# Ten 256-column matmuls read in another order behind each attention product and at every second FFN step

## The chip, the cores and the metric

The kernel runs on one core of a Trainium2 chip. The metric is device time in microseconds for one execution, inputs and outputs in HBM. Times shown are medians of several executions; the profile is of one execution, whose own time stands in the table below.

## What is computed

An attention without a score matrix, then a feed-forward network. Cut to what matters:

```python
# q, k, v: (8, 8, 576, 64) float32; w_in: (512, 2048); w_out: (2048, 512)
q_s = softmax(q, axis=-1)              # over the head's 64 columns
k_s = softmax(k, axis=2)               # over the sequence
kv  = einsum('bhsd,bhse->bhde', k_s, v)
att = einsum('bhsd,bhde->bhse', q_s, kv)
x   = att.transpose(0, 2, 1, 3).reshape(4608, 512)
h   = x @ w_in
out = (h * sigmoid(1.702 * h)) @ w_out   # (4608, 512) float32
```

## The kernel before

**Tiles and blocks.** The 4,608 tokens are worked in nine blocks (t = 0 to 8) of 512. Each block goes through eight steps, and a step takes two of the 16 chunks of 128 of the FFN's inner width. The FFN's matmuls run in float32r, and each product is made of three: high x high, high x low and low x high part of the two operands.

**Two ways of multiplying.** Blocks 0 and 1 compute the first FFN product plainly, in matmuls of 512 columns (`plain1`, line 868), and blocks 0 to 2 do so for the second (`ffn2`, line 1132). From block 2 on the first product (`ffn1`, line 913), and from block 3 on the second (`ffn2s`, line 1048), are taken apart into seven smaller products in Strassen's manner; those matmuls have 256 columns. In `ffn1` the seven products of a step come in the order 1, 5, 6, 3, 7, 2, 4, and each is six matmuls: two halves of the contraction by three operand parts. In `ffn2s` each unit is also six: two row halves by three parts. So the 256-column matmuls come in groups of six on one PSUM region, with 84 matmuls to a step from block 3 on. `ffn1` has 56 steps from block 2 to block 8, which is 2,352 matmuls; `ffn2s` has 2,016.

**Attention among the FFN.** The attention of block t is computed during block t-1: `kv_pairs` multiplies k by v (line 702, matmuls of 64 or 65 columns), `q_tr` transposes q (line 757, four transposes of 128 columns), `x_pairs` applies kv to q (line 778). Where a block of 512 tokens straddles two batches of 576, `x_pairs` splits its columns in two pieces, which are laid out as four runs: a piece of 64 columns is four runs of 16, on input and output. In the plan these three kinds stand between the FFN's groups, some seven places to a block.

**The order of the work.** The order is made by a planner (`Plan`). Each piece of work is added with an engine, an assumed cost, the buffers that it reads and writes, and a rank; the planner plays this through and then emits the pieces in that order, each by calling its `run` function. TensorE is one queue, so its matmuls stand in the order in which the `run` functions were called. A matmul instruction comes with a weight load of its own (LDWEIGHTS, shown as PEld), which loads the 128 x 128 stationary operand. The moving operand is the one whose columns stream through: in `ffn1` it is a part of x, `x[:, r, c, :]`, and in `ffn2s` a part of the weights, `wx[:, r]`, both 128 x 256. The output is 256 neighbouring columns of a PSUM bank.

The other engines split operands into high and low parts (`L1030`, `L1034`), add up the products (`L936`, `L1019`, `L1076`) and apply the activation (`L942`); weights stream in by DMA issued on SyncE and GpSimd (`L411`, `L987`).

Of the kernel before, what the change touches and what calls it, by code (L numbers as in the profile page):

```python
# [136 lines left out]
def efficient_attention_then_gelu_ffn(  # L137
# [27 lines left out]
    nc = tc.nc  # L165
# [136 lines left out]
        nc.tensor.matmul(bank[Z], zeros[:, 0:P], zeros[:, 0:512], start=True, stop=True)  # L302

    plan.fill = 0.3, fill

    def R(t, step, off=0.0):
        return SLOTS * (NS * t + step) + off
# [206 lines left out]
    def parts(t):  # L514
        b, s0 = divmod(t * TB, S)
        n = min(TB, S - s0)
        got = [(b, s0, 0, n // C)]
        if n < TB:
            got.append((b + 1, 0, n // C, P))
        return got  # L520
# [160 lines left out]
    def kv_pairs(b, hps, t, rank):  # L681
        bk = next_bank(t)
        pk = bank[bk][:, : len(hps) * W].rearrange("p (m w) -> p m w", w=W)
        nr[0] += 1
        r = rs[nr[0] % 2][:, : len(hps)]
        reads = ["kl", "vl", "kl0", "vl0", "vt0"]
        for hp in hps:
            reads += [("kt", hp), ("kl", hp), *(early_tile("v", hp)[1] if b == 0 else (("vt", hp),))]

        def run():  # L690
            for m, hp in enumerate(hps):
                vx = early_tile("v", hp)[0] if b == 0 else vt[hp]
                for cols in (slice(0, D), slice(D, W)) if b == 0 else (slice(0, W),):
                    for c in range(CM + 1):
                        for a in range(2):
                            lhs = kt[hp][:, a, c, :] if c < CM else kl[:, 2 * hp + a, :]
                            if c == CM:
                                rhs = vl[:, 2 * hp + a, cols]
                            else:
                                rhs = vl[:, 0, cols] if cols.start == D else vx[:, a, c, cols]  # L700
                            r0 = (a ^ (hp % 2)) * D
                            nc.tensor.matmul(  # L702
                                pk[r0 : r0 + D, m, cols], lhs, rhs, start=c == 0, stop=c == CM, tile_position=(0, r0)
                            )

        def run_r():
            nc.vector.tensor_scalar_add(r, pk[:, :, D], 1e-9)
            nc.vector.reciprocal(r, r)

        PB, RK = ("bank", bk), ("r", nr[0] % 2)  # L710
        plan.add("PE", 0.57 * len(hps) + 0.36, reads, (PB,), rank, run)
        plan.add("DVE", 0.35, (PB,), (RK,), rank, run_r)
        for m, hp in enumerate(hps):

            def run_n(m=m, hp=hp):
                nc.scalar.mul(kvn[b % 2][:, hp, :], pk[:, m, 0:D], r[:, m : m + 1])

            plan.add("ACT", 0.35, (PB, RK), (("kvn", b % 2, hp),), rank, run_n)
# [31 lines left out]
    def q_tr(t, hp, rank):  # L750
        bk = next_bank(t)
        pq = bank[bk]
        qx, QK = q_ready(t, hp)

        def run():
            for c in range(C):
                nc.tensor.transpose(pq[:, c * P : (c + 1) * P], qx[:, c], ident)  # L757

        PB, Q = ("bank", bk), ("qT", hp % 2)
        plan.add("PE", 0.45, (QK, "ident"), (PB,), rank, run)  # L760
        plan.add("ACT", act(TB), (PB,), (Q,), rank, lambda: nc.scalar.copy(qT[hp % 2], pq))

    def x_pairs(t, half, rank):
        hps = (2 * half, 2 * half + 1)
        bks = [next_bank(t) for _ in hps]
        reads = [("qT", 0), ("qT", 1)]
        reads += [("kvn", b % 2, hp) for hp in hps for b, *_ in parts(t)]

        def run():
            for b, s0, p0, p1 in parts(t):  # L770
                for a in range(2):
                    for hp, bk in zip(hps, bks):
                        odd = hp % 2
                        ri, ro = (slice(y * D, (y + 1) * D) for y in (a ^ odd, a))
                        qx, po = (
                            y.rearrange("a (c p) -> a c p", c=C)[:, :, p0:p1] for y in (qT[odd], bank[bk])
                        )
                        nc.tensor.matmul(  # L778
                            po[ro], kvn[b % 2][ri, hp, :], qx[ri], start=True, stop=True,
                            tile_position=((a ^ odd) * D, a * D),  # L780
                        )

        PBs = [("bank", bk) for bk in bks]
        plan.add("PE", 1.2, reads, PBs, rank, run)
        for hp, bk, PB in zip(hps, bks, PBs):
            if t < 2:
                H, L = ((("place", 4 * t + hp), e) for e in "hl")

                def run_l(hp=hp, bk=bk):
                    x = xp(t, hp)  # L790
                    nc.vector.tensor_tensor(out=x[:, 1], in0=bank[bk], in1=x[:, 0].bitcast(F32), op=ALU.subtract)

                plan.add("ACT", act(TB), (PB,), (H,), rank, lambda hp=hp, bk=bk: nc.scalar.copy(xp(t, hp)[:, 0], bank[bk]))
                plan.add("DVE", dve(TB), (PB, H), (L,), rank, run_l)
                continue

            def run_c(hp=hp, bk=bk):
                nc.scalar.copy(xf(half)[:, :, hp % 2, :], bank[bk].rearrange("p (u n) -> p u n", u=2))

            plan.add("ACT", act(TB), (PB,), (("x", half, hp % 2), *taken(t, half)), rank, run_c)  # L800
# [98 lines left out]
    def ffn1(t, step):  # L899
# [4 lines left out]
        def product(n):  # L904
            bk, opens, u, at_ = PROD[n]
            K = ("wt", i, at_) if u == "T" else ("wj", i, u, at_ // 2)

            def run():
                x = xo(n)
                for c in range(2):  # L910
                    for e, (l, r) in enumerate(((0, 0), (0, 1), (1, 0))):
                        w = (wt(i)[:, at_] if u == "T" else wj[i][u][:, at_ // 2])[:, l, c * P : (c + 1) * P]
                        nc.tensor.matmul(  # L913
                            ph[bk], w, x[:, r, c, :],
                            start=opens and c == 0 and e == 0, stop=c == 1 and e == 2, skip_group_check=True,
                        )

            reads = [K, ("xs", n, "h"), ("xs", n, "l")]
            PB = ("bank", bk)
            plan.add("PE", 0.71, reads if opens else [*reads, PB], (PB,), R(t, step, OPS[n][2]), run)  # L920
# [78 lines left out]
    def ffn2s(t, G, rank):  # L999
# [23 lines left out]
        def product(n, src, b, opens):  # L1023
            s = nl[0] % 4
            old = [("gs", s // 2, s % 2, u, jj) for u in range(2) for jj in range(2)] if nl[0] < 4 else []
            nl[0] += 1
            HK, LK = ("L", s, "h"), ("L", s, "l")

            def run_l():
                nc.vector.tensor_tensor(  # L1030
                    out=L[s][:, 1], in0=x[:, :, src], in1=L[s][:, 0].bitcast(F32), op=ALU.subtract
                )

            plan.add("ACT", act(2 * HT), XK(src), (HK, *old), 0, lambda: nc.scalar.copy(L[s][:, 0], x[:, :, src]))  # L1034
            plan.add("DVE", dve(2 * HT), (*XK(src), HK), (LK, *old), 0, run_l)
            PB = ("bank", b)
            for q, p in enumerate(ps):
                if n in CHUNK:
                    K, w = ("wb", ring(n, p)), (ring(n, p), 0, 1)
                else:  # L1040
                    jj, d = {1: (0, 0), 2: (1, 0), 3: (1, 1)}[n]
                    K, w = f"wo{p}{jj}", (p, jj, d)

                def run(q=q, w=w):
                    wx = wo[w[0], w[1]][:, w[2]]
                    for h in range(2):
                        for i, (l, r) in enumerate(((0, 0), (0, 1), (1, 0))):
                            nc.tensor.matmul(  # L1048
                                bv(b)[:, h], L[s][:, l, q, h * P : (h + 1) * P], wx[:, r],
                                start=opens and q == 0 and h == 0 and i == 0, stop=q == 1 and i == 2,  # L1050
                                skip_group_check=True,
                            )

                k, done[0] = done[0], done[0] + 1
                reads = [K, HK, LK]
                plan.add(
                    "PE", 0.71, reads if opens and q == 0 else [*reads, PB], (PB,),
                    R(t, 2 * G + 2 + k // 7, UNITS[k % 7]), run,
                )
                if n in CHUNK and not end:  # L1060
                    load_u(n, pair(t, 2 * G + 2 + q), rank)
                elif n in CHUNK and t + 1 < NB:
                    pass
# [174 lines left out]
```

## Time and profile before

| what | value |
|---|---|
| median of three timed runs | 826.66 us (826.53 to 826.96) |
| the profiled execution's own time | 824.24 us |
| its span, first to last instruction | 822.5 us |
| TensorE busy | 812.3 us, 99% |
| VectorE busy | 671.6 us, 82% |
| ScalarE busy | 587.7 us, 71% |
| matmuls of 256 columns in the FFN | 4,368 |

Reading it: a matmul counts as busy from its start to a modelled end, and neighbours overlap in the pipeline, so a busy TensorE doesn't say how fast its matmuls follow one another. The recorded length of a 256-column matmul is about 0.28 us, while the next one starts about 0.12 us after it. Block 2 begins at about 217 us of the span, and block 3 at about 308 us.

### The profile page before, as it was taken

The page shows a single profiled execution, that of the slowest core. Times are in us where ns is not written, and L with a number is a line of the kernel's source. Part 1 is how long each engine was busy: PE and PEld are TensorE (multiplying, and loading weights), DVE is VectorE, ACT ScalarE, POOL GpSimd, SP SyncE. Part 2 cuts the span into 40 slices and gives each one's busy share as a digit, 9 for nine tenths or more (in the row PEclk, how much of TensorE's full clock was granted, in tenths as well). Part 3 has the DMA queues.
Part 4 walks back from the last instruction along what each step waited for, and adds up shares of the span by engine and source line. Part 5 has one row for each costly group of instructions (what it writes and reads, how often), then busy time and mean ns, then how long its engine had stood idle before and what let it go on. Part 6 is the DMA issues. An engine that isn't in the chain of part 4 may idle for free.

```text
span 822.5 us, 17452 instructions
## 1 busy us (share of the span) xinstructions
PE 812.3 (99%) x6508; PEld 740.4 (90%) x6508; DVE 671.6 (82%) x1292; ACT 587.7 (71%) x1105; POOL 248.8 (30%) x439
## 2 busy tenths in 40 slices
PE   9999999999999999999999999999999999999997
PEld 4677788877888888999999999999999999999997
DVE  8899998799568977978779988899789885686556
ACT  5798969696747796886568895889697755565442
POOL 1120121021222332553234423443343234333430
PEclk9999999999999999999999999999999999999999
DMA  9999753778399978997699868986897589768973
GB/s 280 351 339 318 260 180 128 235 244 277 111 356 270 334 233 236 308 311 217 180 256 355 248 180 233 335 275 184 233 288 222 152 235 286 224 165 247 308 230 103
DMA packets 119061, 204.06 MB, mean 248 GB/s; under 512 B 18624, under 2 KB 63680, under 8 KB 117952
## 3 DMA queue, kind: packets, MB, share of 16 engines
q0 software_dynamic: 53856, 123.23, 52.7%
q1 hardware_dynamic: 65120, 79.71, 30.9%
q8 instruction: 52, 0.85, 0.4%
q14 instruction: 33, 0.27, 0.1%
HBM read 168.30 MB, written 34.60 MB: 247 GB/s over the span
## 4 chain that ended last, share of the span: by engine, by line
PE 92%; DMA 4%; DVE 3%; issue 0%; ACT 0%; SPq 0%; DVEq 0%; ACTq 0%
PE bank L913 33%; PE bank L1048 29%; PE bank L1132 14%; PE bank L868 9%; PE bank L702 2%; PE bank L778 2%; PE bank L757 2%; DMA vl<-in_v 1%; DMA raw<-in_moe_w_out 1%; PE bank L302 1%; DMA out<-O 1%; DMA raw<-in_moe_w_in 1%; DMA qT<-in_v 1%; PE bank L650 0%; PE bank L651 0%; DVE raw L343 0%
## 5 line engine op out<-in xcount | busy, mean ns | idle before, releaser
L913 PE MATMUL bank<-xo,wt 128*128 128x256 f32 x1344 | 193.2, 280 | 0.8 <-ACT X L932 0.8
L913 PEld LDWEIGHTS bank<-xo,wt 128*128 128x128 f32 x1344 | 173.8, 188 | 7.1 <-issue 1.8
L913 PE MATMUL bank<-xo,wj 128*128 128x256 f32 x1008 | 146.2, 281 | 0.0
L1048 PE MATMUL bank<-w,gl 128*128 128x256 f32 x1008 | 140.9, 279 | 0.9 <-DVE O L1076 0.9
L1048 PE MATMUL bank<-w,gh 128*128 128x256 f32 x1008 | 141.3, 279 | 0.2
L411 POOL DMA_DIRECT2D wj<-kept x138 | 73.2, 530 | 214.1 <-PE bank L913 141.5
L913 PEld LDWEIGHTS bank<-xo,wj 128*128 128x128 f32 x1008 | 129.0, 188 | 2.1 <-ACT gl L1034 0.8
L1048 PEld LDWEIGHTS bank<-w,gl 128*128 128x128 f32 x1008 | 127.4, 188 | 1.4 <-issue 1.1
L1048 PEld LDWEIGHTS bank<-w,gh 128*128 128x128 f32 x1008 | 127.5, 188 | 0.7 <-issue 0.3
L936 DVE TENSOR_TENSOR X<-bank,X 128x256 f32<-128x256 f32 x168 | 70.3, 421 | 64.0 <-PE bank L913 60.6
L1132 PE MATMUL bank<-w,gh 128*128 128x512 f32 x384 | 119.8, 393 | 0.8 <-DVE w L379 0.8
L987 POOL DMA_DIRECT2D w<-kept_u x152 | 80.5, 530 | 124.5 <-PE bank L1048 93.5
L932 ACT COPY X<-bank 128x256 f32<-128x256 f32 x168 | 61.6, 371 | 60.0 <-PE bank L913 58.2
L942 ACT ACTIVATE X<-X 128x256 f32<-128x256 f32 x168 | 68.5, 415 | 47.1 <-DVE X L936 46.7
L868 PE MATMUL bank<-xp,wj 128*128 128x512 f32 x384 | 101.0, 397 | 0.9 <-DVE wj L379 0.7
L868 PEld LDWEIGHTS bank<-xp,wj 128*128 128x128 f32 x384 | 71.0, 188 | 20.3 <-issue 2.6
L1076 DVE TENSOR_TENSOR O<-bank,O 128x512 f32<-128x512 f32 x102 | 70.1, 687 | 15.5 <-PE bank L1048 14.8
L1132 PEld LDWEIGHTS bank<-w,gh 128*128 128x128 f32 x384 | 69.4, 188 | 14.2 <-DVE w L379 1.4
L1132 PE MATMUL bank<-w,gl 128*128 128x512 f32 x192 | 75.5, 393 | 0.0
L411 POOL DMA_DIRECT2D wt<-kept_t x84 | 44.5, 530 | 87.3 <-PE bank L913 73.5
L1019 DVE TENSOR_TENSOR X<-X 128x512 f32<-128x512 f32 x96 | 66.2, 695 | 3.7 <-ACT X L942 2.5
L1030 DVE TENSOR_TENSOR gh<-X,gh 128x512 fp32r<-128x512 f32 x84 | 57.5, 686 | 8.1 <-ACT gh L1034 7.8
(125 smaller groups left out, 1205.4 us busy)
## 6 DMA issues: line engine op xcount, KB each, us to landing
wt<-kept_t POOLq DMA_DIRECT2D x84, 512.0 KB, 6.0
w<-kept_u POOLq DMA_DIRECT2D x152, 256.0 KB, 5.5
wj<-kept POOLq DMA_DIRECT2D x126, 256.0 KB, 5.2
kt<-in_k SPq DMA_DIRECT2D x32, 256.0 KB, 6.9
raw<-in_moe_w_in SPq DMA_DIRECT2D x16, 512.0 KB, 8.3
raw<-in_moe_w_out SPq DMA_DIRECT2D x16, 512.0 KB, 6.8
kept<-wj SPq DMA_DIRECT2D x16, 512.0 KB, 5.6
kept_t<-wt SPq DMA_DIRECT2D x8, 1024.0 KB, 4.6
```

The costliest lines, as they stand in the source:

```text
L411: "POOL", 0.6, (key,), to, R(t, step - 2, off), lambda: nc.gpsimd.dma_start(out=out(), in_=src), size=size
L868: nc.tensor.matmul(bank[bk], w[:, c // 2, l, c % 2 * P : (c % 2 + 1) * P], x[:, r], start=c == 0 and e == 0, stop=c == KC - 1 and e == 2)
L913: nc.tensor.matmul(ph[bk], w, x[:, r, c, :], start=opens and c == 0 and e == 0, stop=c == 1 and e == 2, skip_group_check=True,)
L932: vec("ACT", act(HT), (("bank", bk),), (A(n),), slot, lambda: nc.scalar.copy(a(n), ph[bk]))
L936: nc.vector.tensor_tensor(out=a(n), in0=ph[bk], in1=a(n), op=ALU.add)
L942: vec("ACT", act(HT), K, (A(n),), slot, lambda: nc.scalar.activation(a(n), x, AF.Gelu_apprx_sigmoid), "gelu")
L987: nc.gpsimd.dma_start(out=wo[s, 0][:, 1].rearrange("p s f -> p (s f)"), in_=kept_u[p][:, c * DM : (c + 1) * DM])
L1019: nc.vector.tensor_tensor(out=x[:, :, o], in0=x[:, :, n], in1=x[:, :, m], op=op)
L1030: nc.vector.tensor_tensor(out=L[s][:, 1], in0=x[:, :, src], in1=L[s][:, 0].bitcast(F32), op=ALU.subtract)
L1048: nc.tensor.matmul(bv(b)[:, h], L[s][:, l, q, h * P : (h + 1) * P], wx[:, r], start=opens and q == 0 and h == 0 and i == 0, stop=q == 1 an ...
L1076: nc.vector.tensor_tensor(out=half(u, to), in0=bv(b), in1=o, op=ALU.add)
L1132: nc.tensor.matmul(bank[c].rearrange("p (d f) -> p d f", d=2), l, r, start=first_ and e == 0, stop=last and e == 2)
```

## The change

A helper `matmul` takes the place of `nc.tensor.matmul` in `ffn1` and `ffn2s`. It keeps a count of how many matmuls are still to be issued in another order, starting from ten. While the count is above four, the columns of the moving operand and of the output are both walked from last to first. For the last four of the ten, both are walked in eight steps: the 256 columns are seen as two halves of eight runs of 16, and the walk takes the last run of the first half, the last run of the second half, then the runs before them, and so on to the first ones. Input and output are walked alike, so each result lands in its usual place. With the count at zero the matmul is as before.

`again()` puts the count back to ten. It is called when `kv_pairs`, `q_tr` and `x_pairs` emit their matmuls, and at product 1 of every even step of `ffn1`. The number of instructions and the planner's costs are as before.

```diff
@@ -303,6 +303,21 @@
+    BACK, STEPS = 6, 4
+    odd = [BACK + STEPS]
+
+    def matmul(out, w, x, **flags):
+        n = odd[0]
+        odd[0] = max(n - 1, 0)
+        if n > STEPS:
+            out, x = out[:, ::-1], x[:, ::-1]
+        elif n:
+            out, x = (y.rearrange("p (h l f) -> p l h f", h=2, f=16)[:, ::-1] for y in (out, x))
+        nc.tensor.matmul(out, w, x, skip_group_check=True, **flags)
+
+    def again():
+        odd[0] = BACK + STEPS
...
@@ kv_pairs, q_tr and x_pairs alike
         def run():
+            again()
...
@@ -907,12 +925,13 @@ ffn1
             def run():
                 x = xo(n)
+                if n == 1 and step % 2 == 0:
+                    again()
                 for c in range(2):
                     for e, (l, r) in enumerate(((0, 0), (0, 1), (1, 0))):
                         w = (wt(i)[:, at_] if u == "T" else wj[i][u][:, at_ // 2])[:, l, c * P : (c + 1) * P]
-                        nc.tensor.matmul(
-                            ph[bk], w, x[:, r, c, :],
-                            start=opens and c == 0 and e == 0, stop=c == 1 and e == 2, skip_group_check=True,
+                        matmul(
+                            ph[bk], w, x[:, r, c, :], start=opens and c == 0 and e == 0, stop=c == 1 and e == 2
                         )
...
@@ -1045,10 +1064,9 @@ ffn2s
                         for i, (l, r) in enumerate(((0, 0), (0, 1), (1, 0))):
-                            nc.tensor.matmul(
+                            matmul(
                                 bv(b)[:, h], L[s][:, l, q, h * P : (h + 1) * P], wx[:, r],
                                 start=opens and q == 0 and h == 0 and i == 0, stop=q == 1 and i == 2,
-                                skip_group_check=True,
                             )
```

## Rows read from the trace of the kernel before

**Rows 1.** The page: busy time of the engines, the last chain by engine.

```profile
PE 812.3 (99%) x6508; PEld 740.4 (90%) x6508; DVE 671.6 (82%) x1292; ACT 587.7 (71%) x1105; POOL 248.8 (30%) x439
...
PE 92%; DMA 4%; DVE 3%; issue 0%; ACT 0%; SPq 0%; DVEq 0%; ACTq 0%
```

**Rows 2.** Windows of TensorE, two stretches: bounds, us, busy (matmuls), clock, DMA, GB/s.

```profile
330.42:345.77 15.35, 15.35 (x132) 1.00 1.10 298
...
647.61:688.37 40.76, 40.76 (x348) 1.00 0.79 226
```

**Rows 3.** Windows of all engines: busy us (instructions), clock, DMA share, GB/s.

```profile
370.01:416.70 46.69, 46.69 (x414) 46.69 (x413) 38.23 (x66) 27.60 (x62) 14.44 (x27) 1.00 0.71 210
704.37:807.50 103.13, 103.13 (x911) 103.13 (x911) 70.93 (x125) 55.99 (x125) 36.46 (x69) 1.00 0.80 230
449.28:502.78 53.50, 53.50 (x455) 53.50 (x455) 47.71 (x88) 45.71 (x86) 19.59 (x35) 1.00 0.77 229
```

**Rows 4.** Timeline of TensorE: start, length, line, operation, count.

```profile
594.47 0.95 PE L913 MATMUL bank<-xo,wj 128*128 128x256 f32 x6
595.26 0.87 PE L1048 MATMUL bank<-w,gl 128*128 128x256 f32 x6
595.97 0.87 PE L913 MATMUL bank<-xo,wt 128*128 128x256 f32 x6
...
602.86 1.10 PE L778 MATMUL bank<-qT,kvn 64*64 64x448 f32 x16
603.89 0.98 PE L913 MATMUL bank<-xo,wt 128*128 128x256 f32 x6
```

**Rows 5.** Timeline of TensorE, 703 to 705 us.

```profile
703.13 1.09 PE L778 MATMUL bank<-qT,kvn 64*64 64x512 f32 x8
704.15 0.95 PE L913 MATMUL bank<-xo,wt 128*128 128x256 f32 x6
704.94 0.84 PE L1048 MATMUL bank<-w,gl 128*128 128x256 f32 x6
```

**Rows 6.** Timeline, 599 to 600 us, of matmuls (PE) and weight loads (PEld).

```profile
599.12 0.78 PEld L913 LDWEIGHTS bank<-xo,wj 128*128 128x128 f32 x6
599.24 0.87 PE L913 MATMUL bank<-xo,wj 128*128 128x256 f32 x6
...
599.83 0.78 PEld L1048 LDWEIGHTS bank<-w,gl 128*128 128x128 f32 x6
```

**Rows 7.** Timeline, 705 to 706 us: weight loads and matmuls.

```profile
705.51 0.76 PEld L913 LDWEIGHTS bank<-xo,wj 128*128 128x128 f32 x6
705.62 0.84 PE L913 MATMUL bank<-xo,wj 128*128 128x256 f32 x6
```

**Rows 8.** Timeline of TensorE around two short stalls.

```profile
551.50 0.88 PE L913 MATMUL bank<-xo,wj 128*128 128x256 f32 x6
552.22 1.52 PE L1048 MATMUL bank<-w,gl 128*128 128x256 f32 x12
...
560.38 1.53 PE L1048 MATMUL bank<-w,gh 128*128 128x256 f32 x12
561.74 0.88 PE L913 MATMUL bank<-xo,wt 128*128 128x256 f32 x6
562.46 0.87 PE L913 MATMUL bank<-xo,wj 128*128 128x256 f32 x6
```

**Rows 9.** Groups by line and form: count, busy us, mean ns.

```profile
L868 PE MATMUL bank<-xp,wj 128*128 128x512 f32 x384 | 101.0, 397 | 0.9 <-DVE wj L379 0.7 <-ACT X L883 0.2
...
L650 PE MATMUL bank<-kt,ident 128*128 128x512 f32 x8 | 4.4, 632 | 0.0
```

**Rows 10.** Timeline of TensorE, 248 to 251 us, block 2.

```profile
248.13 0.98 PE L913 MATMUL bank<-xo,wj 128*128 128x256 f32 x6
248.94 0.63 PE L1132 MATMUL bank<-w,gh 128*128 128x512 f32 x2
...
250.33 0.84 PE L913 MATMUL bank<-xo,wt 128*128 128x256 f32 x6
```

More of the change, by code (lines that the diff above doesn't have):

```diff
@@ L769, in run @@
         def run():
+            again()
             for b, s0, p0, p1 in parts(t):
@@ L909, in run @@
                 x = xo(n)
+                if n == 1 and step % 2 == 0:
+                    again()
                 for c in range(2):
```

## The prediction

> **What bounds the kernel now.** The page comes first: TensorE is busy for 99% of the span and the chain that ended last runs over it for 92% [rows 1]. The granted clock is 1.00 in the stretches that I looked at, which is the 2.4 GHz level [rows 2, 3]. So the question is not who waits, but how fast one matmul follows the next. A matmul's recorded length doesn't tell that, since neighbours overlap; the distance between starts does, and it comes from dividing a stretch by the matmuls in it. I took the stretches that hold 256-column matmuls alone (lines 913 and 1048, no attention product, nothing idle).
>
> They fall into two sorts. In ten stretches, the first and last of which are shown, and the longest in another view, the pace is about 118 ns: 53.50 us for 455 matmuls, 40.76 us for 348 [rows 2, 3]. In four others it is 113 ns: 46.69 us for 414, 103.13 us for 911 [rows 3]. Clock, line, tiles and the load on the other engines don't separate them: VectorE is busy 82% and 69% of two stretches at 113 ns and 89% of one at 118, and DMA traffic is 210, 230 and 229 GB/s [rows 3]. The pace belongs to the stream and holds for tens of microseconds. I call the two pace 118 and pace 113.
>
> The timeline says where it is set. After four transposes the stream starts again at 594.47, and from the second group on six matmuls take 0.71 us (595.26 to 595.97) [rows 4]; after an attention product at 703.13 it starts again at 704.15, and six take 0.68 us (704.94 to 705.62) [rows 5, 7]. In the timeline such a six shows as 0.87 us or as 0.84, first start to last end. I went through all 40 such restarts behind an attention product: 36 came out at pace 118, four at pace 113. Short stalls inside the stream, behind a late operand, can flip it too: at 551.50 pace 118 becomes 113, with twelve in 1.52 us behind it, and at 561.74 the twelve of 1.53 us end and 0.87 us follows [rows 8]. Counting the starts of all 4,368 matmuls of 256 columns, 2,662 stand at a mean of 117.8 ns, 1,626 at 113.3 and 80 in restarts and stalls. The ten stretches at pace 118 hold some 1,850 of the 2,662; the others stand in shorter runs [rows 4]. The difference is 4.5 ns each, so **2,662 x 4.5 = 12.0 us** is all that the pace can give.
>
> **The change part by part.** It adds no instruction, wait, transfer or byte. The planner's costs are untouched, so the order on every queue stays. What changes is the order in which some 256-column matmuls walk through their columns, on input and output alike, so each sum lands where it did. Replaying the counter over the timeline's order gives 63 sets: 35 behind attention products from 248 us on and 28 at the first product of every second step. Some are cut short by the next product; 390 matmuls go backward and 240 go in eight steps. Up to 216 us there is no 256-column FFN matmul, so nothing changes there.
>
> *Price of the eight steps.* They visit runs of 16 columns. The trace has runs of that length: the attention product that straddles two batches is split into 448 and 64 columns, the latter four runs of 16 on input and output. Its 16 matmuls take 1.03 us from first start to the next group's [rows 4]; the undivided eight with the same columns take 1.02 us [rows 5]. That is 0.6 ns a matmul, and 240 x 0.6 = 0.1 us.
>
> *Price of going backward.* No row shows it. Below: nothing, since it is the same columns. Above: the nearest row for columns that pass at a lower rate is the plain fp32 matmul of line 650, 632 ns against 397 ns for line 868's of the same 512 columns [rows 9]; the difference of 235 ns is 118 ns for 256 columns, 46 us for 390. A loss bound of 118 ns for the eight steps as well would make it 74 us. I take 4.5 ns, the difference between the two paces, because a reversed walk touches the same neighbours in the same groups and the runs of 16 cost nothing visible: 390 x 4.5 = 1.8 us.
>
> The Trainium skill speaks against this part ("Advanced Engine Details and Errata", PSUM Cachelines): a matmul whose output isn't contiguous is said to slow down significantly, while pairs of consecutive elements should stay together. It names no size. The runs of 16 in [rows 4, 5] keep their pairs and show no slowing, so the trace doesn't decide it for a backward walk; by the rule the sum would be the third rival's.
>
> *What a set does to the pace.* In the stream each weight load starts with the matmul before it: the load at 599.83 comes 0.59 us, five paces, after the matmul at 599.24. The matmul follows its load by 0.12 us at pace 118, by 0.11 us at pace 113 [rows 6, 7]. So the pace lies in how load and matmul meet. Block 2 shows what happens when matmuls of another length pass through without idle time: at 248.94 six of 512 columns come in behind a group of 256 at pace 118, and the next group of 256 is at pace 113 [rows 10]. Of the 30 such passages (two with a stall in them left out), six went from 118 to 113, 16 stayed at 118, eight stayed at 113, and **none went from 113 to 118**. That is why I expect a set to help: if an odd order changes a matmul's length or its meeting with the load by a few nanoseconds, it is another length passing through without idle.
>
> How many matmuls it converts: 443 of the positions at pace 118 are the sets themselves, leaving 2,219, or 9.9 us. If a set flips no oftener than a passage (6 of 22), repeated sets turn about half; if it always flips, all. I take 80%, nearer the upper end because a set shifts the meeting up to ten times in two ways: 7.9 us. Sets already at pace 113 change little.
>
> *Cover.* Faster matmuls ask for operands 4% sooner. The stretches at pace 113 show that the other engines deliver: 103.13 us at 113 ns without a stall, with VectorE 69% and ScalarE 54% busy, and 46.69 us with VectorE at 82% [rows 3]. What is late next is a VectorE or ScalarE result at a group's start, as in [rows 8]; each such stall costs tens of nanoseconds, but may flip the pace. The steps' sets are there to meet it.
>
> **Sum.** -7.9 + 1.8 + 0.1 = -6.0 us. From the profiled execution's 824.24 us that gives 818.2. The three timed runs have a median of 826.66, which is 2.4 us above the profiled one; added, it is 820.7.
>
> **The rivals.**
> - *The set acts as a restart does* (slower than before). A restart ended at pace 118 36 times in 40. Then the 35 sets behind attention products change nothing, but those at the steps fall into stretches at pace 113: 371.93 us and 711.06 us are such steps, and some 395 and 850 matmuls behind them in the stretches of [rows 3] would turn to 118, 1,245 x 4.5 x 0.9 = 5.0 us; one in ten of the 2,219 gains, 1.0 us. With no other price: 826.66 + 4.0 = 830.7. It decides where the sets turn more matmuls from 113 to 118 than the other way. For it: stalls of the stream, at 561.74 for one, do end at pace 118. Against it: the 30 passages without idle time, none of which did.
> - *Nothing happens*: the pace hangs on the weight loads, which the change leaves as they are, with their starts. For it: the constant distance from load to matmul in either state [rows 6, 7]. Against: 512-column matmuls with the same loads do flip it. Time: 826.7 plus 0 to 2, at most 828. The Trainium skill bears on it ("TensorE: Matmul & The Clock Gate", LDWEIGHTS): a load's time depends on its columns alone, about 107 ns for 128 by its formula, an estimate that would make the load nearly the whole of pace 113. By that rule the column order of the other operand can't matter; the trace agrees that load and matmul run in step, but not that the pace is one number.
> - *Backward columns pass at a lower rate* (slower): it decides from (7.9 - 0.1) / 390 = 20 ns a matmul on, where the price has eaten the gain. At the bound of 118 ns and with the pace gained: 826.66 - 7.9 + 46 = 865. For it, nothing but that no row shows the walk.
>
> **How the numbers follow.** Steering 0.58 (own range 815 to 824: all 2,662 at no price, and half of them at the full 1.9), nothing 0.14, restart 0.16, lower rate 0.12. A measurement of this kernel tells 0.2%, 1.7 us, from no change. Faster is steering alone, 0.58; slower is restart and lower rate, 0.28; nothing is 0.14. The likeliest gives 820.7. The range goes from 814, the pace gained everywhere at no price, to 833, the restart case with its sets' price; it leaves out the lower rate and little else.
>
> **What would show it.** Right: behind attention products, from the second group of six on, 0.68 us in place of 0.71; the ten stretches at pace 118 now at 113; more 256-column matmuls in the same time, with as many instructions as before and no new idle time. The sets themselves show their price as starts further apart than 118 ns. The restart rival shows 118 ns behind the steps at 371.93 and 711.06. The lower rate shows sets of ten whose starts lie far apart. The prediction is wrong if the odd order leaves the meeting of load and matmul alone, or if its own price per matmul is tens of nanoseconds.

## The result and the profile after

The changed kernel takes 819.65 us (median of four, 817.61 to 821.08) against 826.6 us; the ratio is 0.9915, with a 95% interval of 0.9889 to 0.994. Run again beside the last experiments, on a chip where the kernel before took 826.08 us, it took 817.94 us: 0.991 [0.9892, 0.9928]. So the gain is 0.9%, where 0.7% was forecast.

The profiled execution of the changed kernel took 821.08 us, with a span of 819.3 us. From the page, the span and the busy times, as in [rows 1]:

```profile
span 819.3 us, 17452 instructions
...
PE 807.1 (99%) x6508; PEld 733.3 (90%) x6508; DVE 671.7 (82%) x1292; ACT 586.9 (72%) x1105; POOL 248.8 (30%) x439
```

The number of instructions is the same, TensorE is busy 5 us less, and the other engines do what they did. Windows of TensorE over stretches with 256-column matmuls alone (busy time, matmuls, clock, DMA share, GB/s), beside [rows 2, 3]:

```profile
371.76:418.67 46.91, 46.91 (x413) 1.00 0.72 209
...
635.79:644.86 9.07, 9.07 (x78) 1.00 0.74 179
645.72:685.02 39.30, 39.30 (x347) 1.00 0.78 231
700.95:804.36 103.41, 103.41 (x912) 1.00 0.80 231
```

The stretch from 645.72 us is the one that took 40.76 us in [rows 2]. A window also counts matmuls that reach over its edges; 346 start in it, in both kernels, so they went from 117.8 to 113.6 ns each, sets included. The stretch from 700.95 us was at 113 before and has gained nothing. One stretch, from 635.79 us, is still at 118: 9.07 us for the 77 matmuls that start in it.

The timeline of TensorE behind four transposes, which answers to [rows 4] (all 256-column matmuls now have the helper's line, 316):

```profile
593.12 0.60 PE L774 MATMUL bank<-ident,kt 128*128 128x128 f32 x4
593.48 0.96 PE L316 MATMUL bank<-xo,wj 128*128 128x256 f32 x6
594.27 0.85 PE L316 MATMUL bank<-w,gl 128*128 128x256 f32 x6
594.96 0.84 PE L316 MATMUL bank<-xo,wt 128*128 128x256 f32 x6
595.64 0.84 PE L316 MATMUL bank<-w,gh 128*128 128x256 f32 x6
```

The first six are the backward ones, the next six hold the four in eight steps and two forward; from the third group on six take 0.68 us (594.96 to 595.64). In [rows 4] they took 0.71.

The merged rows hide what happens inside a set. The distances from one start to the next, taken from the same trace's start times in ns, show it; three sets, one behind a restart, one that found the stream at 118, one that found it at 113:

```
found      six backward                  four in eight steps   forward
restart    222 118 117 120 120 120       115 120 117 115       113 113 113 114   (421.36 us)
118        115 118 120 120 120 120       114 120 117 115       113 113 113 114   (373.77 us)
113        117 117 120 120 120 120       114 120 118 115       112 114 113 113   (393.53 us)
```

Whatever a set finds, its backward matmuls settle at 120 ns, its eight-step ones go through the same four distances, and the stream is at 113 behind it. That holds for all 54 sets which no attention product or 512-column matmul interrupts. (Some of the interrupted ones in blocks 2 and 3 go 117, 117, 118, 114 instead.) 49 of the 54 are followed by at least four forward matmuls without a stall, and all 49 go on at 113; below, outcomes are counted over such sets. Of all 4,368 distances, 956 now lie at 116 to 121 ns, where 2,662 did; 467 of the 956 are the sets' own. Of the other 489, 465 stand in nine stretches, each of which begins behind a stall: one or more distances of 163 ns and more.

### The profile page after: what moved, and what is told of

Read it like the earlier page. It is cut to its first block, busy times and chain, and to the rows that moved or that the text cites. A ratio compares the mean times of both kernels' runs of the same rounds, so it can differ in the third digit from the quotient of the medians.

```text
span 819.3 us, 17452 instructions
## 1 busy us (share of the span) xinstructions
PE 807.1 (99%) x6508; PEld 733.3 (90%) x6508; DVE 671.7 (82%) x1292; ACT 586.9 (72%) x1105; POOL 248.8 (30%) x439
## 4 chain that ended last, share of the span: by engine, by line
PE 80%; DMA 9%; DVE 6%; ACT 3%; issue 1%; SPq 1%; POOL 1%; DVEq 0%; POOLq 0%; ACTq 0%
PE bank L316 59%; PE bank L1150 8%; PE bank L886 5%; PE bank L718 2%; DMA vl<-in_v 2%; PE bank L796 2%; PE bank L774 1%; DMA kept<-wj 1%; DMA kept_u<-O 1%; DMA qT<-in_v 1%; PE bank L302 1%; DMA raw<-in_moe_w_out 1%; DMA out<-O 1%; DMA raw<-in_moe_w_in 1%; POOL mx L628 1%
## 5 line engine op out<-in xcount | busy, mean ns | idle before, releaser
L316 PEld LDWEIGHTS bank<-xo,wt 128*128 128x128 f32 x1344 | 172.0, 188 | 8.1 <-ACT X L951 2.1
L316 PE MATMUL bank<-w,gl 128*128 128x256 f32 x1008 | 139.0, 277 | 0.9 <-DVE O L1094 0.9
L316 PE MATMUL bank<-w,gh 128*128 128x256 f32 x1008 | 139.3, 277 | 0.2
```

Source lines behind the costliest of these rows:

```text
L316: nc.tensor.matmul(out, w, x, skip_group_check=True, **flags)
```

## The experiments

Each edit is against the changed kernel. Distances are from the trace's start times. Each ratio is against the kernel before, run beside that experiment; its medians were 825.5 us (e1 to e4), 825.69 (e5 to e8) and 826.08 (e10 to e13).

**Ten backward, none in eight steps** (e1).

```diff
-    BACK, STEPS = 6, 4
+    BACK, STEPS = 10, 0
```

> All ten matmuls of a set go backward, none in eight steps. Two theories. Any order: whatever order differs lets the stream settle anew, mostly at 113 ns; then the sets still end at 113 and the time stays at 819 to 822 us. Two parts: backward matmuls bring the stream to a meeting of their own at 120 ns from whatever it had, and only the eight-step ones lead from there to 113; then the forward matmuls behind a set run at 118, also behind the steps' sets that fell into stretches at 113, and the time is 826 to 832 us.

It took 831.52 us: 1.0071 [1.0044, 1.0098] of the kernel before, slower than both. The backward matmuls settle at 120 as in the change, and then the forward ones go 114, 120, 118, 117, 118: all 49 sets that can be told end at 118, also the one, at 373.03 us, that still found 113. Windows of TensorE over the stretches that answer to those above:

```profile
651.38:692.16 40.78, 40.78 (x347) 1.00 0.77 227
708.46:815.72 107.26, 107.26 (x911) 1.00 0.76 221
```

The longest stretch, 103.13 us in [rows 3], now takes 107.26 us at 118 ns. "Any order" fails here.

**Ten in eight steps, none backward** (e2).

```diff
-    BACK, STEPS = 6, 4
+    BACK, STEPS = 0, 10
```

> All ten matmuls of a set go in eight steps, none backward. Any order: sets end at 113 as often as with both, 819 to 822 us. Two parts: without the common start the outcome depends on the pace before the set; part of the sets end at 118, and the time lies between 820 and 828 us.

826.61 us, 1.0018 [1.0005, 1.0031]: the gain is gone. The eight-step matmuls fall into 114, 120, 117, 115 here too, but reach it at different points, so a set may stop anywhere in the cycle. 36 sets end at 118 and 13 at 113: those that stop behind 120, 117 (or 118), 115 go on at 113, those that stop behind 115, 114 or behind 114, 120 or that never reach the cycle go on at 118.

**No sets at the steps** (e3).

```diff
-                if n == 1 and step % 2 == 0:
-                    again()
```

> The sets behind attention products stay as in the change, those at every second step are left out. Both theories: the runs behind attention products are at 113; a stall that turns the stream to 118 is not mended until the next product. The 28 sets left out cost some 10 x 5 ns each, 1.4 us in all, so 820 to 824 us if stalls turn long stretches, 818 to 820 if they don't.

821.83 us, 0.9951 [0.9936, 0.9966]. The sets behind attention products work as before; behind a stall the stream stays at 118 until the next product. The timeline of TensorE at such a stall (552.06 us), with the groups before and behind it:

```profile
551.33 0.84 PE L316 MATMUL bank<-xo,wj 128*128 128x256 f32 x6
552.06 0.98 PE L316 MATMUL bank<-xo,wt 128*128 128x256 f32 x6
552.88 0.87 PE L316 MATMUL bank<-w,gh 128*128 128x256 f32 x6
...
562.10 0.87 PE L316 MATMUL bank<-xo,wt 128*128 128x256 f32 x6
```

The gain is 0.5% here and 0.9% with both, so about half of it comes from the sets behind the products and the rest from those at the steps.

**Every 256-column matmul backward** (e4).

```diff
-        if n > STEPS:
+        if True:
             out, x = out[:, ::-1], x[:, ::-1]
```

> All 4,368 FFN matmuls of 256 columns go backward, which measures the price of the walk. If backward costs only a pace of 120 ns: 4,368 x (120 - 116.1) = 17 us on the kernel before, 844 us. If the walk costs 4.5 ns on top of either pace, as the prediction took it: 4,368 x 4.5 = 20 us, 846 us, with two paces to be seen. If columns passed at a lower rate: up to 118 ns each, several hundred us more.

839.39 us, 1.0166 [1.0139, 1.0193]. There is one pace, 120 ns, from block 3 to the end:

```profile
654.43:695.95 41.52, 41.52 (x347) 1.00 0.77 223
712.44:821.75 109.31, 109.31 (x912) 1.00 0.75 216
```

(windows of TensorE; 41.52 us for the 346 that start in the first is 120.0 ns). So going backward costs 6.7 ns against pace 113 and 2.2 against 118. That is no lower rate for columns: the distance is 2% longer than at pace 118. The time stayed under the 844 us that I gave; the distances sum to 15.8 us more than in the kernel before, where I had 17.

**Only the input backward, and only the output backward** (e5, e6). In the six, one of the two operands stays forward.

```diff
         if n > STEPS:
-            out, x = out[:, ::-1], x[:, ::-1]
+            x = x[:, ::-1]            # e5
+            out = out[:, ::-1]        # e6, in another kernel
```

> In the six backward matmuls of a set only the input is read from last to first; the output is written forward, so those columns of the sums land in the wrong place. Which side makes the 120 ns? If the read does: the six still settle at 120 and the sets end at 113, 818 to 821 us. If the write does: the six run at the pace that they found, the four in eight steps start from no common point, and part of the sets end at 118, 822 to 827 us.

> The mirror image: in the six only the output is written from last to first and the input is read forward, so those columns of the sums land in the wrong place. If the write makes the 120 ns, 818 to 821 us with sets ending at 113; if the read does, 822 to 827 us with outcomes that differ from set to set.

One execution each: 821.2 us with the input alone, 831.18 us with the output alone. Behind four transposes, as above, in the two timelines of TensorE; first the input alone:

```profile
509.41 0.96 PE L316 MATMUL bank<-xo,wj 128*128 128x256 f32 x6
510.21 0.85 PE L316 MATMUL bank<-w,gl 128*128 128x256 f32 x6
510.90 0.84 PE L316 MATMUL bank<-xo,wt 128*128 128x256 f32 x6
```

Then the output alone:

```profile
511.14 0.95 PE L316 MATMUL bank<-xo,wj 128*128 128x256 f32 x6
511.93 0.87 PE L316 MATMUL bank<-w,gl 128*128 128x256 f32 x6
512.63 0.87 PE L316 MATMUL bank<-xo,wt 128*128 128x256 f32 x6
```

With the input alone the distances are those of the change (200, 117, 120, 120, 120, 120, then 114, 120, 118, 115, then 113), and again all 49 sets end at 113. With the output alone the six run at 117 to 120, or at 113 where a restart came out at 113, as forward ones do; one of 49 sets ends at 113. So for the six it is the order in which the input is read; the two sides of the eight-step walk were not taken apart. The 831 us are above what I gave for that case: only 351 distances are left at 110 to 115 ns, of 1,626 in the kernel before.

**Six backward, five in eight steps** (e7).

```diff
-    BACK, STEPS = 6, 4
+    BACK, STEPS = 6, 5
```

> Six backward and five in eight steps, one more than in the change. Any order: one more makes no difference, 818 to 822 us. Two parts with a cycle: the eight-step matmuls go through 114, 120, 117, 115 ns again and again, and only a set that ends with the cycle leads to 113; the fifth breaks it, nearly every set ends at 118, and the time is 828 to 831 us as for ten backward ones.

831.1 us, 1.0064 [1.0047, 1.0081]: one more eight-step matmul to a set, and the gain is gone. The sets go 114, 120, 117, 115, 114 and then, forward, 123, 112, 119, 117, 118. All 49 end at 118. Behind four transposes again; from the third group on six take 0.70 us:

```profile
510.53 0.96 PE L316 MATMUL bank<-xo,wj 128*128 128x256 f32 x6
511.32 0.86 PE L316 MATMUL bank<-w,gl 128*128 128x256 f32 x6
512.03 0.86 PE L316 MATMUL bank<-xo,wt 128*128 128x256 f32 x6
512.73 0.87 PE L316 MATMUL bank<-w,gh 128*128 128x256 f32 x6
```

**Six backward, eight in eight steps** (e10).

```diff
-    BACK, STEPS = 6, 4
+    BACK, STEPS = 6, 8
```

> Six backward and eight in eight steps: two whole cycles of 114, 120, 117, 115 ns. If what counts is that a set ends with the cycle, the sets end at 113 as with four; the four further matmuls cost 4 x 3.2 ns in each of 63 sets, 0.8 us, so 819 to 822 us. If more eight-step matmuls than four spoil it whatever their number, 828 to 831 us as with five.

818.33 us, 0.9909 [0.9892, 0.9925]: the gain is back, a little more of it than the 819 to 822 us that I gave. The sets go through the cycle twice, and all 49 end at 113. Behind four transposes; the second cycle ends in the third group, and the fourth is 0.84 us long, where it was 0.87 with five:

```profile
443.81 0.96 PE L316 MATMUL bank<-xo,wj 128*128 128x256 f32 x6
444.60 0.86 PE L316 MATMUL bank<-w,gh 128*128 128x256 f32 x6
445.30 0.85 PE L316 MATMUL bank<-xo,wt 128*128 128x256 f32 x6
445.99 0.84 PE L316 MATMUL bank<-w,gl 128*128 128x256 f32 x6
```

**Three backward, a set at every step** (e8).

```diff
-    BACK, STEPS = 6, 4
+    BACK, STEPS = 3, 4
...
-                if n == 1 and step % 2 == 0:
+                if n == 1:
```

> Three backward and four in eight steps, and a set at every step instead of every second. Two parts: three suffice to reach 120 from either pace, so sets still end at 113; 35 sets behind attention products save 3 x 7 ns each, 0.7 us; stalls are mended after one step, worth some 1.1 us of the 494 matmuls still at 118 outside the sets; the other sets cost 56 x 29 ns = 1.6 against 1.4 us. Together 1 to 2 us less than the change, 817 to 820 us, if six aren't needed; if six are, outcomes differ and it is 821 to 826 us.

828.3 us, 1.0033 [1.002, 1.0045]; my forecast missed. Three aren't enough. A set that found 118 mostly goes 115, 117, 120 and then 116, 116, 117, 117, and stays at 118. Of the 22 whose second and third were both within a nanosecond of 120, 21 reach the cycle and end at 113. In all, 49 of the sets with their four complete end at 118 and 23 at 113. A single 120 is not yet the common point.

**Forward only, one matmul split in two** (e11). The first matmul of a set is split into two of 128 columns; no order is changed.

```diff
-        if n > STEPS:
-            out, x = out[:, ::-1], x[:, ::-1]
-        elif n:
-            out, x = (y.rearrange("p (h l f) -> p l h f", h=2, f=16)[:, ::-1] for y in (out, x))
+        if n == BACK + STEPS:
+            start, stop = flags["start"], flags["stop"]
+            nc.tensor.matmul(out[:, 0:128], w, x[:, 0:128], skip_group_check=True, start=start, stop=stop)
+            nc.tensor.matmul(out[:, 128:256], w, x[:, 128:256], skip_group_check=True, start=False, stop=stop)
+            return
         nc.tensor.matmul(out, w, x, skip_group_check=True, **flags)
```

> No matmul goes in another order. In place of a set, its first matmul alone is split into two of 128 columns, each with its own weight load, all forward. The prediction's reason was that any matmul of another length which passes without idle time can turn 118 into 113. If so, part of the sets end at 113 and the time is 820 to 826 us, the 63 further matmuls costing some 60 ns each. If only the two orders together lead there, the stream stays as in the kernel before, 826 to 831 us.

832.09 us, 1.0083 [1.0061, 1.0105], above both of my ranges. The further matmul costs nearly a whole pace, some 102 to 113 ns in the stream, not 60: the two halves take 58 and 111 ns, and the matmul behind them 169. In the stream, a split that found 118 ended at 113 six times in 15, and one that found 113 stayed there seven times in seven, as the passages of [rows 10] do. Behind an attention product 39 of 40 end at 118, much as plain restarts do (36 of 40). The timeline of TensorE at a split (lines 314, 315) that turned 118 into 113:

```profile
435.11 1.22 PE L317 MATMUL bank<-w,gh 128*128 128x256 f32 x9
436.17 0.22 PE L314 MATMUL bank<-xo,wj 128*128 128x128 f32 x1
436.23 0.27 PE L315 MATMUL bank<-xo,wj 128*128 128x128 f32 x1
436.34 0.79 PE L317 MATMUL bank<-xo,wj 128*128 128x256 f32 x5
436.97 0.84 PE L317 MATMUL bank<-w,gl 128*128 128x256 f32 x6
```

**Sets at steps 4 and 7 only** (e12), and **the change again** (e13).

```diff
-                if n == 1 and step % 2 == 0:
+                if n == 1 and step in (4, 7):
```

> As the change, but the sets away from attention products come at steps 4 and 7 of a block instead of 0, 2, 4 and 6. In the changed kernel's trace the stalls that turn the stream to 118 lie at steps 3 to 5 of block 3 and at the start of step 7. 14 sets fewer save 14 x 50 ns = 0.7 us, the stalls at step 7 are mended at once (some 275 matmuls, 1.2 us), one stall at step 5 is mended later (0.4 us): 1.5 us less than the change, 816 to 819 us beside the change's 818 to 821 in the same call. If the stalls move with the pace, no difference.

> The changed kernel again, beside the others on one chip: 818 to 821 us, 0.7 to 1.1% under the kernel before.

e12 took 820.18 us, 0.9929 [0.9913, 0.9944]; e13 817.94 us, 0.991 [0.9892, 0.9928]. So moving the sets gains nothing. The sets work where they stand, but stalls at other steps then leave the stream at 118 until the next product, from 474 to 504 us and from 559 to 589 us in its trace. It was to be 1.5 us faster than the change and wasn't. No version tried here beats the change by more than the noise; e10 is level with it.

## Why the prediction was right, point by point

**The pace is what counts, and 4.5 ns a matmul is what it can give.** Right. Between the two profiled executions the 4,368 distances sum to 516.1 us before and 510.6 after, 5.5 us less; in the repeat (e13) they sum to 508.8, 7.3 us less. I forecast 6.0 less.

**How many are converted.** The number was right, the reason was not. I took 80% of the 2,219 matmuls outside the sets, since a set might fail to flip the pace. After, 956 - 467 = 489 stand at 118, so 78% were converted (84% in the repeat, e13). But no set that can be told failed; what is left at 118 stands behind stalls that come between the sets. Outside the sets the matmuls take 6.2 us less than in the kernel before, 7.9 in the repeat, where I had 7.9.

**The price of a set.** Too high, and wrongly split. The sum added 1.9 us on top of what stood at the sets' places. Place by place, the sets' matmuls take 0.6 us more than the same matmuls did before, in the changed kernel and in the repeat: the 390 backward ones 0.7 more, the eight-step ones (244, not 240) nothing. The backward price of 4.5 ns is 6.7 against pace 113 and 2.2 against 118 (e4), and most of the places stood at 118. The eight steps cost 3.2 ns each against pace 113 (466 / 4 - 113.3), not the 0.6 that the split attention product suggested, but 1.3 less than pace 118. Only a set that found 113 is dear: 117 + 117 + 4 x 120 for the six and 466 ns for the four, 47 ns more than ten at 113. In the profiled execution the gain was 1.7 us less than forecast and the price 1.3 us less; that the sum came so close is in part luck.

**Why a set helps.** Here the reasoning fell short, though the sign came out. "Another length passing through without idle" does what the passages showed: e11 flips 6 of 15 from 118 to 113 and none back. But it would make a set a matter of chance that can't harm. In fact the sets' outcome is fixed by their counts: with 6 and 4, and with 6 and 8, all 49 end at 113; with 6 and 5, none; with ten backward, none, and stretches that stood at 113 are turned to 118. The sentence that sets already at pace 113 change little holds where the eight-step matmuls end with their cycle, as with 6 and 4. The picture that fits all the runs: backward reading has one meeting of load and matmul, at 120 ns, which six matmuls reach from anywhere and three don't; eight-step reading has a cycle of four meetings; forward reading has two that hold, at 113 and 118, and which of them it takes follows from what ran just before. The six erase what was there, the four lead to the point from which forward reading goes to 113.

**The restart rival.** It didn't happen: the 16 sets that found 113 all left it at 113. Ten backward matmuls do what the rival said, and turn those stretches to 118; they took 6.0 us more than the kernel before beside them, where I had 4.0 without a price of the sets.

**Nothing happens.** It fell. The weight loads are untouched in e4 and e5, and the pace follows the input's order all the same. The distance from load to matmul is itself what changes, 110, 115 or 117 ns at pace 113, 118 and 120. By the formula of "TensorE: Matmul & The Clock Gate" (LDWEIGHTS) in the Trainium skill a load of 128 columns takes about 107 ns, an estimate; all three paces lie above it, and it doesn't tell them apart. (The trace records 188 ns for a load.)

**Backward columns at a lower rate.** It fell: 2.2 to 6.7 ns, not tens. On the rule of "Advanced Engine Details and Errata" (PSUM Cachelines) in the Trainium skill, that output which isn't contiguous slows a matmul significantly: output walked backward alone ran at the pace of forward output (e6). For this walk the measurement and the rule differ.

**What the profiled time hides.** The profiled execution fell from 824.24 to 821.08 us only, while the median fell by 7. Its first 256-column matmul starts at 218.39 us, where it started at 216.87: 1.5 us were lost before anything that the change touches. The 512-column matmuls' distances sum to 228.6 us against 226.1, 1.6 of the 2.5 us ahead of that first 256-column matmul. In the repeat that sum is 226.2 us, and the execution 817.94 us.

## What to carry to other kernels

When an engine is full, look at the distance between starts by stretch, not at the busy share or the mean length: two paces of one instruction, 4% apart, show only there. Where a stream has more than one steady pace, a few instructions that force one known meeting and leave it at one known point can choose the pace, but the count is part of the method: a fifth eight-step matmul undid it. No other kernel was tried, so whether six and four do it elsewhere is not shown. Judge such a change by the sets' outcomes in the trace, since unrelated waiting hid half of it in one profiled execution.

## What was not expected of the hardware

- The pace of a stream of weight load and 256-column float32r matmul depends on the order in which the moving operand is read: 113 or 118 ns forward, 120 backward, a cycle of 114, 120, 117 and 115 in runs of 16 (116.5 on the mean), all at a granted clock of 1.00.
- The order in which the output is written made no difference that shows for the backward walk (e6: 117 to 120 ns, or 113 where a restart came out at 113).
- The outcome repeats from set to set, within a nanosecond or two: 49 of 49 at 113 with four eight-step matmuls, 49 of 49 at 118 with five.
- Why the forward stream has two paces stays open. The runs show that what ran just before decides it; no run here looked at what makes the difference.
